# A Fourier filter and MLP mixer: new queues for the first batch's inputs, twelve buffers for the first token weights, and the rounding of weights moved within the prologue

## The chip, the cores and the metric

One core of one Trainium2 chip. The metric is the device time of one execution in microseconds (us), of which several are taken. All executions used below were of the fast state; a ratio is the mean time of one kernel's fast runs over the mean of the other's of the same rounds on the same chip, so it is not quite the ratio of the medians quoted. "Span" is the length of the one execution that was profiled.

## The reference

```python
# x: (8, 3008, 256); filt_r, filt_i: (1505, 256)
X = np.fft.rfft(x, axis=1)
y = np.fft.irfft(X * (filt_r + 1j * filt_i), n=3008, axis=1)      # per channel
# token mixing, then channel mixing; w_tok1 (3008, 256), w_tok2 (256, 3008),
# w_ch1 (256, 1536), w_ch2 (1536, 256)
h = np.maximum(y.transpose(0, 2, 1) @ w_tok1, 0.0) @ w_tok2
u = y + h.transpose(0, 2, 1)
out = u + np.maximum(u @ w_ch1, 0.0) @ w_ch2
```

## The kernel before

The length-3008 transform is split into length-64 and length-47 parts. The first of the eight batches goes through the filter alone, as a prologue; the others are filtered beside the mixer of the batch before. Beside the first batch's filter the weights are also prepared: token weights w1 (twelve tiles) and w2 (twelve tiles), and the channel weights, are loaded into staging buffers and rounded, each in three steps (`begin` loads, `copy` and `end` round).

```python
BY_PE = 6       # so many w2 tiles are added up by TensorE (identity matmuls), the rest on VectorE
EARLY = 12

def filt_load(c, first):                       # the filter pieces of table c
    q = nc.gpsimd if first else nc.sync
    for src, i, p0 in ((filt_r, 0, 0), (filt_i, 1, HALF)) + (...):
        q.dma_start(t[p0:p0 + A, i], raw(src, k0, ...))
        # ... three more pieces on q

early = [(up, "u")] * 2 + [(tp, "t")] * 2 + [(vp, "v")] * 2
late = [(t2p, "t2"), (t3p, "t3")]
stages = [(t4p, "t4")] * (A // 2) + early * 3 + late * 5   # which buffer stages which weight tile

def convert():                                 # one more weight tile rounded, one more load begun
    ended[0] += 1
    while behind and behind[0][0] < ended[0] - 2:
        behind.pop(0)[1]()
    advance(end); advance(copy); advance(begin)

def x_load(b, c):                              # one input tile, two halves
    where, tag = ((xp, "x"), (tp, "t"), (vp, "v"))[c % 3] if b == 0 else (xp, "x")
    # ... both halves on nc.sync

# prologue: the twelve length-64 units of batch 0, then its filter units
for i, _ in enumerate(dft(GROUPS[0])):
    if i == 0:
        for t, src in ((wai_t, wait_d), (wa, wa_d), (wai, wai_d), (ident, ident_d)):
            nc.scalar.dma_start(t, src)
    if i < NXC:                                # NXC = 12
        if i in (0, 2, 4, 6):  advance(begin)
        if i == 5:             advance(copy)
        if i in (7, 9, 11):    convert()       # three tiles rounded here
    elif (i - NXC) % 3 == 2:   convert()       # and one every third filter unit
    # ...
for i in range(rounds, A // 2 + TC * N2 // NG):
    convert()                                  # the rest; the token sums begin at a given i
    if i == A // 2 + BY_PE - 1:
        sum_up()
        acc = token_sums(0)
h1s[0] = token_relu(acc)
```

## Time and profile before

| | before |
|---|---|
| time, median (range), 4 runs beside the changed kernel | 2587.94 us (2585.22 to 2590.66) |
| span, TensorE busy | 2587.2 us, 97% |
| transposes start / last filter product / token sums start / first mixer sums | 31.14 / 122.15 / 136.93 / 166.40 us |
| first to last filter product ("stage 3") | 72.6 us |
| from the first mixer sums to the end ("the rest") | 2420.8 us |

TensorE is nearly always busy from the first mixer sums on. The prologue is therefore read from left to right, as a row of stages, each with the wait that ends it. The prediction below shows the lines. Below, "first mixer sums" is the first `v<-u` of VectorE, as there.

### The profile page before, as it was taken

The numbers are of one execution on the slowest core, as the hardware profiler recorded it, in microseconds if no ns is written. First come the engines' busy times: TensorE is split into PE (matmuls) and PEld (weight loads), VectorE is DVE, ScalarE is ACT, GpSimd is POOL, SyncE is SP. The second block draws the span as 40 slices with busy tenths as digits, with TensorE's granted clock in tenths as the row PEclk, the third lists the DMA queues.
The fourth block names the chain that finished last, engine by engine and source line by source line (L and its number), as shares of the span: only waits on it lengthen the run. The fifth ranks groups of instructions, "written<-read, shape, count | busy, mean of one in ns | idle before, by whom it ended". The sixth has DMA issues, their size and how long they took to land.

```text
span 2587.2 us, 31459 instructions
## 1 busy us (share of the span) xinstructions
PE 2505.6 (97%) x10952; PEld 2000.9 (77%) x10952; DVE 1816.0 (70%) x3458; ACT 691.2 (27%) x1347; POOL 526.9 (20%) x966
## 2 busy tenths in 40 slices
PE   5989999999999999999999999999999999999998
PEld 2556666788878777888787777788888888888887
DVE  6897888556675888746666788846678577647676
ACT  2433222123221222222321222212222122212222
POOL 3652211111211112112112111121121121211212
PEclk7999999999999999999999999999999999999999
DMA  6964333312232332202232233211232121100001
GB/s 167 232 195 155 109 106 103 106 48 90 90 90 64 88 88 71 80 17 89 90 96 77 75 84 87 80 31 57 90 85 75 50 64 53 25 9 8 17 12 21
DMA packets 151834, 205.20 MB, mean 79 GB/s; under 512 B 34216, under 2 KB 102034, under 8 KB 151676
## 3 DMA queue, kind: packets, MB, share of 16 engines
q1 hardware_dynamic: 81068, 115.65, 15.7%
q0 software_dynamic: 30656, 39.93, 6.4%
q10 hardware_dynamic: 39952, 47.61, 5.7%
q8 instruction: 87, 1.43, 0.2%
q14 instruction: 71, 0.58, 0.1%
HBM read 131.23 MB, written 71.83 MB: 78 GB/s over the span
## 4 chain that ended last, share of the span: by engine, by line
PE 78%; DVE 13%; issue 3%; DMA 3%; ACT 2%; SPq 0%; ACTq 0%; POOL 0%; DVEq 0%; POOLq 0%
PE ps_po L631 26%; PE ps_pg L597 15%; PE ps_pg L613 11%; PE ps_b L540 4%; PE ps_b L557 4%; DVE t L575 3%; DVE hh L575 3%; PE ps_acc L540 2%; PE ps_acc L557 2%; PE ps_acc L494 2%; PE ps_b L562 2%; PE ps_acc L417 2%; DVE u L575 2%; DVE s L575 1%; PE ps_b L470 1%
## 5 line engine op out<-in xcount | busy, mean ns | idle before, releaser
L575 DVE TENSOR_TENSOR hh<-ps_pg,s 128x512 f32<-128x512 f32 (+3 forms) x864 | 482.4, 586 | 624.4 <-ACT s L600 623.8
L676 POOL DMA_DIRECT2D out_dram<-r x757 | 409.8, 550 | 1949.1 <-ACT hh L618 929.0
L618 ACT ACTIVATE hh<-hh 128x512 f32<-128x512 f32 (+1 forms) x576 | 348.0, 621 | 1122.8 <-DVE hh L575 1122.8
L631 PE MATMUL ps_po<-t,wc 128*128 128x256 f32 (+1 forms) x2304 | 535.5, 375 | 5.4 <-DVE t L575 4.6
L631 PEld LDWEIGHTS ps_po<-t,wc 128*128 128x128 f32 x2304 | 434.5, 190 | 132.9 <-issue 53.3
L631 PE MATMUL ps_po<-hh,wc 128*128 128x256 f32 (+1 forms) x1728 | 413.2, 375 | 3.1 <-POOL wc L339 2.8
L597 PE MATMUL ps_pg<-v,wc 128*128 128x256 f32 (+1 forms) x1728 | 413.3, 375 | 0.2
L631 PEld LDWEIGHTS ps_po<-hh,wc 128*128 128x128 f32 x1728 | 327.5, 190 | 42.4 <-POOL wc L339 3.6
L597 PEld LDWEIGHTS ps_pg<-v,wc 128*128 128x128 f32 x1728 | 326.9, 190 | 40.5 <-DVE v L575 3.0
L613 PE MATMUL ps_pg<-u,wc 128*128 128x256 f32 (+1 forms) x1152 | 294.5, 378 | 7.0 <-DVE hh L575 6.5
L575 DVE TENSOR_TENSOR t<-t,hh 128x256 f32<-128x256 f32 (+1 forms) x576 | 242.0, 420 | 19.8
L613 PEld LDWEIGHTS ps_pg<-u,wc 128*128 128x128 f32 x1152 | 216.2, 190 | 43.5 <-DVE hh L575 17.4
L575 DVE TENSOR_TENSOR s<-ps_pg,hh 128x512 f32<-128x512 f32 (+1 forms) x288 | 196.0, 681 | 30.7 <-DVE hh L575 0.9
L575 DVE TENSOR_TENSOR t<-hh 128x512 f32<-128x512 f32 (+1 forms) x288 | 192.7, 669 | 0.6 <-ACT hh L618 0.6
L597 PE MATMUL ps_pg<-u,wc 128*128 128x256 f32 (+1 forms) x576 | 169.9, 377 | 1.6 <-DVE hh L575 1.6
L613 PE MATMUL ps_pg<-v,wc 128*128 128x256 f32 (+1 forms) x576 | 169.2, 375 | 0.0
L600 ACT COPY s<-ps_pg 128x256 f32<-128x256 f32 (+1 forms) x288 | 106.0, 368 | 154.7 <-PE ps_pg L597 151.5
L613 PEld LDWEIGHTS ps_pg<-v,wc 128*128 128x128 f32 x576 | 108.9, 190 | 13.3
L597 PEld LDWEIGHTS ps_pg<-u,wc 128*128 128x128 f32 x576 | 102.7, 191 | 20.3 <-issue 8.8
L540 PE MATMUL ps_b<-t,w 128*128 128x256 f32 x480 | 106.3, 384 | 4.3 <-DMA t<-g_tmp 4.3
L557 PE MATMUL ps_b<-w,h 128*128 128x512 f32 (+1 forms) x232 | 107.8, 587 | 0.0
L540 PEld LDWEIGHTS ps_b<-t,w 128*128 128x128 f32 x480 | 92.2, 192 | 17.9 <-issue 4.0
(102 smaller groups left out, 2251.4 us busy)
## 6 DMA issues: line engine op xcount, KB each, us to landing
g_tmp<-t ACTq DMA_DIRECT2D x128, 192.0 KB
x<-in_x_dram SPq DMA_DIRECT2D x184, 128.0 KB
out_dram<-r POOLq DMA_DIRECT2D x698, 32.0 KB, 1.8
z_tmp<-t ACTq DMA_DIRECT2D x84, 256.0 KB
t<-z_tmp SPq DMA_DIRECT2D x112, 192.0 KB
t<-g_tmp SPq DMA_DIRECT2D x42, 512.0 KB
wb<-wbi_t SPq DMA_DIRECT2D x80, 224.0 KB
filt<-in_filt_r_dram SPq DMA_DIRECT2D x128, 48.0 KB
```

The source lines that it names most:

```text
L417: nc.tensor.matmul(ps, wa0 if b == 0 else wa, xs.pop((b, c)).rearrange("p a d -> p (a d)"), start=True, stop=True)
L494: nc.tensor.matmul(ps[0:KR], wbs[k // WC][:, k % WC, P:], p, start=(i == 0), stop=(i == len(parts) - 1))
L540: nc.tensor.matmul(acc[:, t, :], w1[:, a, ts(t, P)], t4[b, a // TC4][:, a % TC4, :], start=(a == 0 and t == 0), stop=(a == A - 1 and t == ...
L557: nc.tensor.matmul(ps[:, 0:w], h1[:, t, ts(dh, P)], w2[:, t, ds(m * 512, w)], start=(t == 0), stop=False)
L562: nc.tensor.matmul(ps[:, ds(q * P, n)], t4[b, c][:, r, ts(dh, P)], wai[:, 0:n], start=False, stop=(q == 3))
L575: nc.vector.tensor_tensor(out=out, in0=in0, in1=in1, op=op)
L597: nc.tensor.matmul(ps[:, 0:hw], chan[0][:, jp, n, :], mov, start=True, stop=True)
L600: nc.scalar.copy(out=s[:, 0], in_=g[0][:, 0, 0:hw])
L613: nc.tensor.matmul(ps[:, 0:hw], chan[0][:, jp, n, :], mov, start=True, stop=True)
L618: nc.scalar.activation(out=hs, in_=hs, func=AF.Relu)
L631: nc.tensor.matmul(po[i][:, j, 0:hw], chan[1][:, jp, n, :], mov, start=(jp == 0 and first == 1), stop=(jp == JP - 1 and last == 1))
L676: q.dma_start(rows[g, e, :, ds(h * A + 4 * m, n)], blocks[ts(g, CW), h, e, 0:n])
```

## The change

The intent: the first batch's input goes ahead of all else, half of it from ScalarE's queue; twelve buffers let all w1 loads start beside the length-64 units; nothing is rounded there. The filter pieces of the first batch, all on GpSimd before, are split between SyncE and GpSimd; more w2 tiles are added up by TensorE.

```diff
-BY_PE = 6
-EARLY = 12
+BY_PE = 8
+BY_PE_LAST = 3
+BESIDE = 13
 def filt_load(c, first):
-        q = nc.gpsimd if first else nc.sync
         for src, i, p0 in ((filt_r, 0, 0), (filt_i, 1, HALF)) + ...:
+            q = nc.gpsimd if first and i else nc.sync
-    early = [(up, "u")] * 2 + [(tp, "t")] * 2 + [(vp, "v")] * 2
-    late = [(t2p, "t2"), (t3p, "t3")]
-    stages = [(t4p, "t4")] * (A // 2) + early * 3 + late * 5
+    round_ = [(p_, t_) for p_, t_ in ((up, "u"), (tp, "t"), (vp, "v"), (t2p, "t2")) for _ in range(2)]
+    stages = [(t4p, "t4")] * 7 + round_ * 3 + [(t2p, "t2"), (t3p, "t3")] * 5
 def w1_load(i):
-        q = nc.sync if i < EARLY else nc.gpsimd
+        q = nc.sync
 # w2_load
-        if i < BY_PE:
+        if i < BY_PE or i >= TC * N2 // NG - BY_PE_LAST:
 # convert: loads begin by a count, up to 7 (at last 4) ahead, instead of one per call
-        advance(begin)
+        while begun[0] < len(tiles) and begun[0] < ended[0] + (4 if begun[0] >= len(tiles) - len(LAST) else 7):
+            start()
 def x_load(b, c):
-        where, tag = ((xp, "x"), (tp, "t"), (vp, "v"))[c % 3] if b == 0 else (xp, "x")
+        where, tag = ((xp, "x"), (t1p, "t1"), *round_[0::2])[c // 2] if b == 0 else (xp, "x")
+            q = nc.scalar if b == 0 and h else nc.sync
 # dft: the first input is all issued ahead; the three first filter tables follow at once
-        ahead = 3 * XB if first else XB
+        ahead = NXC if first else XB
-            if first and i in (5, 8):
-                w_load(i // 6)
+            if first and i < FB:
+                w_load(i)
 # prologue
-                if i in (0, 2, 4, 6):
-                    advance(begin)
-                if i in (7, 9, 11):
-                    convert()
+                if i >= FB:
+                    for _ in range(2 if i < 6 else 1):
+                        start()
 # ... 13 tiles are rounded evenly beside the filter units; sum_up() also before token_relu
```

More of the change, by code (lines that the diff above doesn't have):

```diff
@@ L378, in advance, with start @@
             next(s, None)
+    begun = [0]
+    def start():
+        advance(begin)
+        begun[0] += 1
     def sum_up():
@@ L405, in x_load @@
             lo = h * A + c * XC
-            nc.sync.dma_start(t[h * HALF:(h + 1) * HALF, 0:n, :], rows[:, lo:lo + n, :])
+            q = nc.scalar if b == 0 and h else nc.sync
+            q.dma_start(t[h * HALF:(h + 1) * HALF, 0:n, :], rows[:, lo:lo + n, :])
             if n < XC:
-                nc.sync.dma_start(t[h * HALF:(h + 1) * HALF, n:XC, :], rows[:, lo:lo + 1, :])
+                q.dma_start(t[h * HALF:(h + 1) * HALF, n:XC, :], rows[:, lo:lo + 1, :])
         xs[b, c] = t
@@ L517, in dft @@
                 b_unit(k)
-                if k % KC == 0 and k // KC + 2 < K2 // KC:
+                if k % KC == 0 and k // KC + 2 < K2 // KC and (k or not first):
                     t2_load(k // KC + 2)
@@ L771 @@
             nc.vector.memset(t, 0.0)
-        rounds = 0
         second = dft(GROUPS[1])
@@ L779 @@
             if i < NXC:
-                if i in (0, 2, 4, 6):
-                    advance(begin)
-                if i == 5:
+                if i >= FB:
+                    for _ in range(2 if i < 6 else 1):
+                        start()
+                if i == NXC - 1:
                     advance(copy)
-                if i in (7, 9, 11):
+            else:
+                k = i - NXC - 2
+                if k >= 0 and (k + 1) * BESIDE // (K2 + 1) > k * BESIDE // (K2 + 1):
                     convert()
-                    rounds += 1
-            else:
-                if (i - NXC) % 3 == 2:
-                    convert()
-                    rounds += 1
-                k = i - NXC - 2
                 if 19 <= k < 25:
@@ L805 @@
         chan.extend((both[:, 0], both[:, 1]))
-        for i in range(rounds, A // 2 + TC * N2 // NG):
+        for i in range(BESIDE, A // 2 + TC * N2 // NG):
             convert()
-            if i - rounds < XB:
+            if i - BESIDE < XB:
                 next(second)
@@ L812 @@
                 acc = token_sums(0)
+        sum_up()
         h1s[0] = token_relu(acc)
```

## The prediction

> **What bounds the kernel now.** I read the page first (busy shares, then the 40 slices), then a table of windows cut at the stages of the start, then the timeline of those stages.
>
> ```profile
> PE 2505.6 (97%) x10952; PEld 2000.9 (77%) x10952; DVE 1816.0 (70%) x3458; ACT 691.2 (27%) x1347; POOL 526.9 (20%) x966
> ...
> PE   5989999999999999999999999999999999999998
> ```
>
> TensorE is busy 97% of 2587 us, and nearly all that is missing lies in the first slices of 65 us each. So the change can win only what the start (the "prologue") wastes; from the first mixer step on, every matmul waits for the one before it, and a later first step is a later end. The windows give the stages; the columns are length, then busy time of PE, PEld, DVE, ACT, POOL, then granted clock, DMA share, GB/s:
>
> ```profile
> 0.00:31.14 31.14, 18.04 (x26) 6.10 (x27) 11.22 (x17) 9.97 (x16) 11.06 (x24) 0.85 0.91 227
> 31.14:48.20 17.06, 1.76 (x4) 0.52 (x2) 17.00 (x16) 1.79 (x3) 0.00 (x0) 0.60 0.49 109
> 48.20:122.15 73.95, 67.59 (x233) 39.41 (x233) 63.57 (x140) 33.04 (x68) 48.14 (x87) 0.97 0.81 209
> 122.15:136.90 14.75, 11.30 (x32) 5.53 (x33) 11.19 (x25) 9.07 (x16) 2.76 (x5) 1.00 1.01 259
> 136.90:159.60 22.70, 22.64 (x96) 19.33 (x96) 21.53 (x46) 4.01 (x7) 10.55 (x20) 0.92 0.84 220
> 159.60:166.40 6.80, 6.14 (x26) 3.61 (x26) 4.81 (x10) 2.91 (x5) 1.07 (x3) 1.00 0.00 1
> 166.40:225.00 58.60, 47.37 (x173) 32.36 (x172) 52.73 (x91) 20.26 (x37) 43.22 (x71) 0.94 0.53 166
> 225.00:2587.00 2362.00, 2330.73 (x10366) 1894.10 (x10366) 1633.96 (x3117) 610.16 (x1195) 410.04 (x758) 1.00 0.24 69
> ```
>
> These are: (1) the twelve length-64 units, with batch 0's input coming in; (2) sixteen transposes on VectorE, TensorE idle; (3) 32 filter units with weight tiles rounded between them; (4) what is left before the token sums; (5) the token sums; (6) the steps up to the mixer's first sums; (7) the mixer's start, paced by VectorE, which still rounds ten weight tiles; (8) the steady mixer. Idle TensorE time is 13 + 15 + 6 + 3.5 us in the first four stages and 11 us in the seventh. All of it is 49 us, under 2% of the time, so a gain over 2% is out of reach.
>
> The timeline shows who ends each stage:
>
> ```profile
> 9.55 0.59 ACT L419 COPY turned<-ps_acc 128x512 f32<-128x512 f32 x1 [2.29 <-DMA wai_t<-wait_t]
> ...
> 28.44 2.04 PE L417 MATMUL ps_acc<-x,turned 128*128 128x512 f32 x2 [2.57 <-DMA x<-in_x_dram]
> ...
> 31.14 17.00 DVE L455 STREAM_TRANSPOSE turned<-turned 128x512 f32<-128x512 f32 x16 [1.87 <-ACT turned L419]
> ...
> 136.93 22.64 PE L540 MATMUL ps_b<-t,w 128*128 128x256 f32 x96 [3.40 <-DMA t<-g_tmp]
> ...
> 159.61 0.60 ACT L546 ACTIVATE h<-ps_b 128x512 f32<-128x512 f32 x1 [5.34 <-PE ps_b L540]
> 160.26 1.98 PE L557 MATMUL ps_acc<-w,h 128*128 128x512 f32 x4 [0.69 <-ACT h L546]
> 166.40 0.92 DVE L575 TENSOR_TENSOR v<-u 128x512 f32<-128x512 f32 x1 [1.75 <-ACT u L564]
> ```
>
> The last input tile reaches TensorE at 28.4; the transposes need all twelve tiles, so they start at 31.1. The token sums start 14.8 us after the last filter product (122.15). The first row shows ScalarE held 2.3 us in its own queue: a transfer that it issues waits for an earlier one to land.
>
> **What the Trainium skill says.** "DMA: Bandwidth & Descriptors", section "Issuing engines are not separate DMA queues": transfers started from several engines run on the same 16 DMA engines, so a second queue saves "the time on the sequencer it takes to initiate the DMA". The trace agrees that there is little more to have: one queue issues 128 KB each 0.64 us, 205 GB/s, and the core moved 247 to 264 GB/s between 10 and 25 us. "TensorE: Matmul & The Clock Gate", "What's actually happening": after an idle window of about 3.4 us the clock halves until it has been busy that long. Here, after 2.97 us idle, the input matmul pair took 2.05 us and two more 1.9 and 2.0, against 1.02 to 1.12 warm; the granted clock from 20 to 25 us was 0.51. "ScalarE: Activation LUTs", "What ACT_TABLE_LOAD costs": about 1283 ns for the load; the trace shows 1.28 us.
>
> **The change, part by part.** The engine-by-engine instruction lists of both kernels, with their waits, give the order; the durations are the trace's.
>
> *Inputs first, on two queues.* The input is 3.1 MB; first data at about 4 us as now, then some 250 GB/s with 0.3 MB of filter beside it: last tile at about 16.5 instead of 28.4. But half of the transfers are now issued by ScalarE, ahead of its table load and of the copies that empty PSUM. In the compiled list each queue has four completion semaphores here: ScalarE's fifth input transfer waits for its first to land, and so on. So ScalarE issues its last one when tile 8 has landed (13.3), ends at 13.9, loads the table (15.2), makes copy 0 (15.8), and then has the four constant tables to issue, which wait for the last input tiles and for a filter piece that the other queue issues behind a 224 KB table: about 18.4 (estimate). Only then do copies 1 to 11 run. TensorE has two banks, so it stands at unit 3 until about 19. Nine units at 0.95 warm are 8.6, plus about 1.2 for a cold restart, plus copy 0.6: transposes start at about **29.5**, not 31.1. Most of the 12 us won in the DMA is given back.
>
> *No rounding there.* Three tiles leave stage 1, where VectorE was idle anyway (11.2 of 31.1 busy). Stage 3 before: 32 units at 1.345 (three products, with gaps) + nine 512-wide roundings at 2.26 + two 377-wide at 1.95 = 67.3, against 72.6 from first product to last, so 5.3 of waits, most for filter pieces on the shared GpSimd queue. After: 43.0 + 12 x 2.26 = 70.2, with filter halves on two queues and the w1 tiles loaded beforehand, so I give it 2.0 of waits: 72.2. Last filter product at 29.5 + 17.0 + 1.4 + 72.2 = **120.1** (before 122.15).
>
> *Twelve buffers.* They take the w1 loads out of stage 3 and let w2 loads start earlier; that is in the 2.0.
>
> *More tiles on TensorE.* Eight w2 tiles must now be rounded between the last product and the token sums instead of five (BY_PE 8, and two fewer done before). Before, the five took 12.25 with 2.9 of waits, and the sums started at 14.8, held by the reload of g_tmp. After: 12.25 + 3 x 1.84 + about 0.7 of further wait on ScalarE's order = 18.5, then the last tile's two matmul pairs, 1.3 to 1.5: **20.0** (+5.2). The sums take 22.7 as before. Behind them TensorE now has three more w2 tiles, 3 x 1.27 = 3.8, and in ScalarE's list their copies, about 1.2, stand before the activation that lets it go on; VectorE saves five additions at 0.85 but is waiting by then. So sums to first mixer step: 6.8 + 5.0 = **11.8**.
>
> Sum: 120.1 + 20.0 + 22.7 + 11.8 = 174.6 against 166.4, **+8.2 us**. Stages 7 and 8 have the same instructions, so the end moves with it: 2588.2 + 8.2 = 2596.
>
> **Rivals.**
> (a) *ScalarE does not hold up stage 1*, because its transfers land sooner than I think, and TensorE follows the arrivals. Transposes at 20 to 22, 8 to 9 us sooner than above: the total is then about 2587, and with no waits in stage 3 about 2585. For it: this is plainly the intent, and DMA busy was 0.91 in that stage with w1 in it. Against it: ScalarE's order and waits, and the 2.29 us that it already lost with only four transfers.
> (b) *VectorE is the only bound after stage 1*, and the work taken from it shows as gain: five additions at 0.85 are 4.3 us. For it: it is busy 86% of stage 3 and 95% of stage 5. Against it: it had 1.75 us to spare at 166.4, and TensorE's in-order queue puts the sums between it and the end. It would make 2584 to 2588.
> (c) *The DMA queues bind instead*: twelve w1 tiles (6.2 MB, 25 us at 250 GB/s) stand before the fourth filter table in the in-order queue, and w2 loads bunch after stage 3. It costs 3 to 6 us more: about 2600.
>
> **Range and chances.** My sum says 2596; the misjudgement I fear most, (a), lies wholly below, and (c) is less likely, so I take **2594 us**, 8 in 10 between **2581 and 2603**. Two per cent would be 52 us, more than all idle time of the start: faster 0.01, same 0.98, slower 0.01.
>
> **What would show it.** In the profile after: last input tile landed at 16 to 18; ScalarE's second copy into the turned tile not before 17; transposes from 28 to 31 (at 22 or earlier, rival a); first to last filter product 72 us with waits of 2 (over 76, rival c); token sums 20 us after the last product; six identity matmul groups between the sums and the activation; VectorE idle before it. If the mixer's first sums come before 166, I am wrong in stage 1 or in the order after the sums; if they come at 174 and the end does not move, the mixer's start had slack that I have not seen.

## The result, and the profile after

The changed kernel takes 2615.56 us (median of 4 runs, 2613.96 to 2616.15) against 2587.94 on the same chip: ratio 1.0106, 95% interval 1.0088 to 1.0123. The class "within 2%" was right. The time was not: 2615.6 lies 12.6 us above the range, and the loss is 27 us where 6 were expected.

The windows of the changed kernel, cut at the same events (columns as in the prediction):

```profile
0.00:30.22 30.22, 16.86 (x24) 5.71 (x24) 4.50 (x5) 8.25 (x14) 6.28 (x15) 1.00 0.87 226
30.22:47.28 17.06, 0.00 (x0) 0.00 (x0) 17.00 (x16) 1.67 (x3) 0.00 (x0) 0.63 0.72 170
47.28:136.08 88.80, 71.56 (x229) 41.72 (x229) 66.66 (x144) 32.70 (x67) 26.23 (x47) 0.88 0.67 174
136.08:154.95 18.87, 18.62 (x49) 8.25 (x50) 14.88 (x34) 11.23 (x20) 4.01 (x8) 1.00 0.89 250
154.95:175.83 20.88, 20.88 (x98) 18.40 (x97) 16.85 (x36) 4.40 (x9) 5.19 (x10) 1.00 0.34 107
175.83:187.09 11.26, 9.94 (x38) 5.53 (x37) 5.84 (x11) 5.64 (x10) 2.71 (x6) 1.00 0.11 33
```

The third row holds the loss. VectorE works 3.1 us more there than before, but the row is 14.9 us longer, and DMA is busy only 0.67 of it: everything waits, and the wire (the 16 DMA engines that all queues share) isn't full. Stage by stage, with the step of the prediction beside it (differences to the kernel before, us):

| stage | predicted | measured |
|---|---|---|
| start of the transposes | -1.6 | -0.9 (30.22) |
| first to last filter product | -0.4 (72.2) | **+14.9 (87.5)** |
| last product to token sums | +5.2 (20.0) | +4.1 (18.9) |
| token sums | 0 | -1.7 (20.9) |
| sums to first mixer sums | +5.0 (11.8) | +4.5 (11.3) |
| first mixer sums to the end | 0 | **+6.5 (2427.3)** |
| span | +8.2 | +27.2 |

Stage 3 first. The waits of the changed kernel between 47 and 136 us; columns: engine and line, what it waited for, us in total, times, longest. First SyncE's queue, then VectorE, then ScalarE, then TensorE:

```profile
SPq L302 <- DMA g_tmp<-t: 23.1, 2, 17.9
...
DVE p L492 <- PE ps_pg L480: 6.3, 5, 2.0
DVE p L492 <- PE ps_b L480: 6.0, 1, 6.0
DVE p L492 <- ACT filt L226: 4.2, 2, 2.4
...
ACT filt L226 <- DMA filt<-in_filt_r_dram: 21.4, 6, 9.2
...
PE ps_b L480 <- DMA wb<-wbi_t: 9.2, 3, 7.4
```

(SyncE's row is of 30 to 136 us.) In the kernel before, the same list has no w1 load that waits for `g_tmp` at all (`L301` is the w1 load there, `L302` here), and shorter waits of VectorE:

```profile
SPq L301 <- DMA st<-in_moe_w_tok_dram: 1.4, 2, 0.7
...
DVE p L482 <- PE ps_pg L470: 2.2, 5, 0.7
DVE p L482 <- ACT filt L225: 2.0, 2, 1.7
```

So a load of weights, which needs nothing but a free buffer, stood for 17.9 us because of the write of a result of the first filter units. The timeline shows what stood behind it: SyncE's queue, then the engines that wanted what it brings.

```profile
30.50 32.91 SPq L302 DMA_DIRECT2D st<-in_moe_w_tok_dram  x11
63.51 0.54 SPq L445 DMA_DIRECT2D wb<-wbi_t  x1
64.16 0.32 SPq L214 DMA_DIRECT2D filt<-in_filt_r_dram  x1
...
53.19 0.33 ACTq L515 DMA_DIRECT2D g_tmp<-t  x1
...
66.63 1.22 PE L480 MATMUL ps_b<-turned,wb 128*128 128x256 f32 x2 [7.45 <-DMA wb<-wbi_t]
...
67.24 0.62 ACT L226 COPY filt<-filt 64x512 f32<-64x512 f32 x1 [9.21 <-DMA filt<-in_filt_r_dram]
```

The last eleven w1 transfers (each tile takes two) keep SyncE 33 us, though one issue takes some 0.5; only then come the fourth filter table (`wb`, 63.51) and its real pieces (64.16), and TensorE and ScalarE stand for 7.5 and 9.2 us. The compiled instruction lists say why a load waits for a result. A transfer reports that it has landed on a completion semaphore. SyncE's loads and ScalarE's writes use the same eight of them, handed out in turn, and each transfer first waits for the one that used its semaphore last:

```
the changed kernel's lists (place, line, transfer, what it waits for)
ScalarE   32 L515 DMACopy g_tmp<-t_304 96x2x256 [waits DMAHW0_49,Activation_49]
ScalarE   36 L515 DMACopy g_tmp<-t_341 96x2x256 [waits DMAHW4_49,Activation_49]
SyncE     44 L302 DMACopy st<-in_moe_w_tok_dram 64x512 [waits DMAHW0_49]
SyncE     48 L302 DMACopy st<-in_moe_w_tok_dram 64x256 [waits DMAHW4_49]
SyncE     49 L445 DMACopy wb<-wbi_t 128x448 [waits DMAHW5_49,PE_49]
```

The trace's instruction records have the same: eight semaphores for the two queues, and SyncE's 46th and 50th transfers (places 44 and 48 of the list) waiting for those that the two `g_tmp` writes count on. Semaphore 0 had gone last to the first `g_tmp` write, which ScalarE issues at 53.19, when the first filter units are done. So load 44, whose turn came at 37.5 when load 43 had been issued, stood until that write had landed, 55.35; in this time the DMA engines were only 0.33 busy, so it isn't the volume that it waits for. Load 48 stood likewise until 62.95 for the second write, issued at 58.06; there they were 0.92 busy, with the four w1 transfers just let go. Behind it comes the fourth filter table, place 49.

The rest next. About 2 of its 6.5 us come in the first 60 us of the mixer (the same step of VectorE comes 1.9 us later than before, counted from the first mixer sums; the second batch's token activation comes 359.0 us after the first batch's, before 357.2); later batches agree. The other 4.3 come after the last output is issued. The last transfers of GpSimd, of the changed kernel:

```profile
2604.34 2.72 POOL L686 DMA_DIRECT2D out_dram<-r  x5 [13.48 <-issue]
```

They end at 2607.06, and the span at 2614.4; in the kernel before they end at 2584.19, and the span at 2587.2. No view of the profile shows work in between. The trace's instruction records, which also hold what the views leave out, have one DRAIN instruction of GpSimd there: 3.08 us long before, 7.42 after. All other engines have finished 4.5 us before it ends; in the kernel before, 0.2 us.

### The profile page after: what moved, and what is told of

Read it like the earlier page. It is cut to its first block, busy times and chain, and to the rows that moved or that the text cites. A ratio compares the mean times of both kernels' runs of the same rounds, so it can differ in the third digit from the quotient of the medians.

```text
span 2614.4 us, 31473 instructions
## 1 busy us (share of the span) xinstructions
PE 2517.4 (96%) x10972; PEld 2008.0 (77%) x10972; DVE 1811.9 (69%) x3451; ACT 694.2 (27%) x1354; POOL 501.5 (19%) x917
## 4 chain that ended last, share of the span: by engine, by line
PE 77%; DVE 14%; issue 3%; DMA 2%; ACT 2%; POOL 1%; ACTq 0%; DVEq 0%; SPq 0%; POOLq 0%
PE ps_po L641 26%; PE ps_pg L607 15%; PE ps_pg L623 11%; PE ps_b L550 4%; PE ps_b L567 4%; DVE t L585 3%; DVE hh L585 3%; PE ps_acc L550 2%; PE ps_acc L567 2%; PE ps_acc L504 2%; PE ps_b L572 2%; PE ps_acc L427 2%; DVE u L585 2%; DVE s L585 2%; PE ps_b L480 1%
## 5 line engine op out<-in xcount | busy, mean ns | idle before, releaser
L504 PE MATMUL ps_acc<-p,wb 128*96 128x256 f32 (+1 forms) x256 | 98.0, 485 | 11.7 <-ACT t L510 5.5
```

Source lines behind the costliest of these rows:

```text
L504: nc.tensor.matmul(ps[0:KR], wbs[k // WC][:, k % WC, P:], p, start=(i == 0), stop=(i == len(parts) - 1))
```

## The experiments

All twelve kernels computed the right result. In the table, "to the end" is the time from the first mixer sums to the end, "GpSimd's transfers" are counted in the trace, and the last column is how long after GpSimd's last transfer its DRAIN ended.

| kernel | median us | ratio to before (95%) | transposes | stage 3 | to sums | after sums | first mixer sums | to the end | GpSimd's transfers | DRAIN |
|---|---|---|---|---|---|---|---|---|---|---|
| before | 2587.9 | | 31.1 | 72.6 | 14.8 | 6.8 | 166.4 | 2420.8 | 901 | 2.2 |
| changed | 2615.6 | 1.0106 (1.0088-1.0123) | 30.2 | 87.5 | 18.9 | 11.3 | 187.1 | 2427.3 | 852 | 6.5 |
| e1 w1 tail on GpSimd | 2606.4 | 1.0063 (1.0048-1.0078) | 29.0 | 75.6 | 18.9 | 11.3 | 174.0 | 2426.4 | 862 | 7.5 |
| e2 old staging buffer | 2613.0 | 1.0093 (1.0078-1.0108) | 30.1 | 84.7 | 18.9 | 11.3 | 184.2 | 2426.0 | 852 | 6.5 |
| e3 input all on SyncE | 2615.7 | 1.0100 (1.0085-1.0115) | 22.7 | 94.4 | 18.6 | 11.3 | 186.2 | 2427.3 | 852 | 6.5 |
| e4 no w2 tile after the sums | 2611.3 | 1.0086 (1.0069-1.0102) | 30.5 | 87.0 | 18.5 | 6.8 | 182.1 | 2425.5 | 852 | 6.5 |
| e6 nine w1 tiles begun | 2605.0 | 1.0063 (1.0048-1.0078) | 30.1 | 77.3 | 18.9 | 11.3 | 176.8 | 2425.7 | 852 | 6.5 |
| e5 four edits | 2610.5 | 1.0082 (1.0067-1.0097) | 32.8 | 83.3 | 18.9 | 6.8 | 181.0 | 2427.4 | 862 | 7.5 |
| e5b, input half on GpSimd | 2595.4 | 1.0030 (1.0014-1.0047) | 20.0 | 78.9 | 18.9 | 6.8 | 163.9 | 2428.9 | 875 | 8.7 |
| e7, six w2 tiles on TensorE | 2610.2 | 1.0081 (1.0066-1.0097) | 32.0 | 82.5 | 15.2 | 11.5 | 180.6 | 2426.8 | 862 | 7.5 |
| e8 real filter halves back | 2598.3 | 1.0042 (1.0027-1.0057) | 29.5 | 73.6 | 18.6 | 11.3 | 172.3 | 2424.4 | 901 | 2.2 |
| e9 = e5b with filters back | 2582.9 | 0.9981 (0.9965-0.9998) | 20.2 | 73.5 | 18.5 | 6.8 | 158.3 | 2422.0 | 924 | 2.8 |
| e10 input on SyncE, nine tiles | 2588.3 | 1.0003 (0.9989-1.0018) | 22.7 | 74.9 | 18.9 | 6.8 | 162.5 | 2424.5 | 901 | 2.2 |
| e11 input half on GpSimd, nine tiles | 2582.7 | 0.9981 (0.9966-0.9996) | 20.5 | 74.9 | 18.9 | 6.8 | 160.4 | 2421.4 | 914 | 2.6 |

The kernel before, run beside them, had medians of 2587.5 to 2589.3 us. Each edit below is against the changed kernel.

**e1: the last five w1 tiles from GpSimd's queue.** Theory: the w1 loads in SyncE's queue are what stage 3 waits for.

```diff
-        q = nc.sync
+        q = nc.sync if i < 7 else nc.gpsimd
```

> The changed kernel with the last five of the twelve w1 tiles loaded from the GpSimd queue, not the SyncE queue. Theory A (shared completion semaphores): the SyncE queue stands for 17.9 us before w1 load 20 and again before load 24, because each takes over the completion semaphore of a g_tmp write that ScalarE issues only after the first filter products; the fourth filter table stands behind them. Without these loads in that queue the gap of 6 to 7 us after the eighth filter product goes, first to last filter product is 80 us or less instead of 87.5, and the total falls by 6 to 12 us. Rival B (the 6.2 MB of w1 simply keep the DMA engines busy): the gap stays within 2 us. Rival C (later stalls around 120 to 131 us have the same cause): then first to last product falls to 76.

Stage 3 fell from 87.5 to 75.6 us and the time by 9.2. The w1 loads that stay in SyncE's queue no longer wait for `g_tmp`, and the longest single wait of a filter product was 1.4 us. The 75.6 is what rival C had named: the later stalls go too. So 12 of the 15 us need the w1 loads in that place; that they need the filter pieces behind them as well is shown by e8.

**e2: the old staging buffer for one w2 tile.** Theory: the time after the first mixer sums is longer because of which buffer stages which late weight tile.

```diff
-    stages = [(t4p, "t4")] * 7 + round_ * 3 + [(t2p, "t2"), (t3p, "t3")] * 5
+    stages = [(t4p, "t4")] * 7 + round_ * 2 + round_[0:6] + [(t3p, "t3")] + [(t2p, "t2"), (t3p, "t3")] * 5
```

> The changed kernel with the staging buffers of the last rounds drawn in another order, so that the first late channel tile is not staged in the buffer that the second channel tile of the early list still holds. Theory D: GpSimd's in-order queue stood 21.8 us for that buffer, issued its channel-weight loads only at 184.4, and its sums for the first channel tiles came 3.9 us later; this is most of the 6.4 us that the mixer's start lost beyond the later first step. Expected: first mixer sums at 187 as in the changed kernel, but the wait of TensorE for GpSimd's sums (3.0 us) gone and the total 3 to 6 us below the changed kernel. Rival: the mixer's start is bound by VectorE anyway and the total stays within 1.5 us.

The theory fell: the rest went from 2427.3 to 2426.0, a fifth of what was to be explained. The wait that it named, TensorE's 3.0 us for GpSimd's sums, did go; a wait of 3.0 us for VectorE took its place, as the rival had it. The time is not distinguishable from the changed kernel's (the intervals overlap).

**e3: the whole first input from SyncE.** Theory: ScalarE's waits for its own input transfers hold up the length-64 units.

```diff
-            q = nc.scalar if b == 0 and h else nc.sync
+            q = nc.sync
```

> The changed kernel with all of the first batch's input on the SyncE queue. Theory E (ScalarE's issuing holds up its own copies): the transposes start at 20 to 22 us instead of 30.2 although the last input tile lands 1 to 3 us later. Rival (TensorE or the DMA engines bound stage 1): transposes at 28 or later. The total need not follow, since the stall of the SyncE queue in the filter units ends with the g_tmp writes: if it keeps its length, the total falls by 7 to 10 us.

The transposes start 7.5 us sooner, 22.72 instead of 30.22, as the theory has it. And nothing is won: stage 3 becomes 94.4, and the first mixer sums come at 186.2 instead of 187.1. TensorE gets the fourth filter table at the same time as in the changed kernel (66.63):

```profile
66.27 1.22 PE L480 MATMUL ps_b<-turned,wb 128*128 128x256 f32 x2 [14.76 <-DMA wb<-wbi_t]
```

TensorE arrives 7.5 us earlier and waits 7.3 us longer. The wait for the semaphore did move: ScalarE issues its second `g_tmp` write at 50.38 instead of 58.06, and SyncE goes on at 54.77 instead of 62.95. But then eight w1 transfers of 256 KB still stand before the table, where the changed kernel had one left:

```profile
54.77 4.94 SPq L302 DMA_DIRECT2D st<-in_moe_w_tok_dram  x8
59.80 0.53 SPq L445 DMA_DIRECT2D wb<-wbi_t  x1
```

The DMA engines are 0.81 busy from 55 to 60 us and fully busy from 60 to 66.3. So here volume took what the shorter wait gave, and that both tables land at the same time is chance. A gain is worth nothing while other loads stand before the transfer that is waited for; this is why stage 1 had to be judged together with stage 3.

**e4: no w2 tile left to TensorE behind the token sums.**

```diff
-BY_PE_LAST = 3
+BY_PE_LAST = 0
```

> The changed kernel with no w2 tile joined on TensorE behind the token sums (BY_PE_LAST 0 instead of 3). Theory F: token sums' end to the mixer's first sums falls from 11.4 to about 7 us, total 3 to 5 us less. Rival: VectorE, with three additions of 0.83 more, becomes the bound there, and the total stays within 1.5 us.

After the sums 6.8 us pass instead of 11.3, so these three tiles cost 4.5 us there. The timelines show it. The changed kernel has six groups of identity matmuls and their copies in ScalarE's order before the activation that starts the next step, at 180.27, 4.4 us after the sums end (175.83). Without them it starts as soon as the sums end (175.32). First the changed kernel, then e4:

```profile
175.67 0.80 PE L285 MATMUL ps_po<-both,ident 128*128 128x377 f32 x2
...
179.66 0.81 ACT L288 COPY w<-ps_po 128x192 f32<-128x192 f32 x2 [0.42 <-PE ps_po L286]
180.27 0.62 ACT L556 ACTIVATE h<-ps_b 128x512 f32<-128x512 f32 x1
```

```profile
175.32 0.60 ACT L556 ACTIVATE h<-ps_b 128x512 f32<-128x512 f32 x1 [5.18 <-PE ps_b L550]
```

**e6: nine w1 tiles begun in stage 1 instead of twelve, the queues unchanged.** Here the rest of the loads come behind the fourth to sixth filter tables. It is to separate the order in the queue from the volume.

```diff
-                    for _ in range(2 if i < 6 else 1):
-                        start()
+                    start()
```

> Only nine instead of twelve w1 tiles are begun beside the length-64 units; no queue is changed. The loads that stood in the in-order SyncE queue behind a busy completion semaphore come later then, after the fourth and fifth filter tables. Theory (order): what costs is that those loads stand ahead of the filter tables while they wait for a semaphore that a slow write of ScalarE's queue holds; then the stall of some 18 us in the SyncE queue is gone or falls where nothing is needed, stage 3 (first to last filter product) is 76 to 79 us instead of 87.5, and the total is 2605 to 2609. Rival (volume): the 6.2 MB of w1 ahead of the tables is what costs, so that three tiles less take away only a quarter of the 15 us: stage 3 is 83 to 85, total 2611 to 2613.

Stage 3 is 77.3, in the range of the order theory and far from that of volume. The same three tiles on the same queue cost 10 us less when they come later.

**e5, e5b, e7: the parts put together.** e5 takes the edits of e1, e2, e3 and e4. e5b has GpSimd in e3's edit (`q = nc.gpsimd if b == 0 and h else nc.sync`). e7 is e5 with `BY_PE = 6`.

> Four edits at once: last five w1 tiles from GpSimd's queue, the old staging buffer for one w2 tile, the whole first input from SyncE, no w2 tile left to TensorE after the sums. If the parts found so far are independent and add up: transposes at 22.7, stage 3 76 us, sums 18.5 after the last product, first mixer sums 6.8 after the sums, so at about 163 (before 166.4), and with the 6.4 us that the rest is longer (2427 against 2421) the total is 2590 (2587 to 2592), level with the kernel before. Rival (each gain is given back in the next stage, as with the input on one queue alone, where 7.5 us won in stage 1 were lost in stage 3): stage 3 is 82 or more, first mixer sums after 169, total 2595 to 2600.

> As the run with four edits, but the second half of the first input is issued by GpSimd instead of SyncE. If ScalarE's waits alone cost stage 1 its 7.5 us, two queues without ScalarE do as well as one or a little better: transposes at 21 to 23, the rest as there, total within 2 us of that run. Rival: GpSimd's queue is slower to issue or its own copies of constants come late, and the transposes start at 25 or later.

> As the run with four edits, and six instead of eight w2 tiles go to TensorE before the token sums. Theory: the 4 us that stage 4 gained are the extra tiles that must be rounded before the sums may start; with two fewer, the sums start 14.5 to 15.5 us after the last product instead of 18.5, and the total is 3 us below that run if VectorE keeps pace. Rival: VectorE's additions for those two tiles come back in the sums, which then last 22.5 instead of 20.9, and behind them, so that the first mixer sums come no sooner than 1 us before that run's.

e5 missed by 20 us: its transposes start at 32.8, not at 22.7. Each edit alone was as expected, and the sum was not. The timeline of TensorE in its stage 1 shows input tiles that arrive late:

```profile
25.78 2.05 PE L427 MATMUL ps_b<-x,turned 128*128 128x512 f32 x2 [1.45 <-DMA x<-in_x_dram]
30.05 2.05 PE L427 MATMUL ps_acc<-x,turned 128*128 128x512 f32 x2 [2.23 <-DMA x<-in_x_dram]
```

In e3 the w1 loads stood behind the input in one queue, the first issued at 24.6 us, so the input had the wire; in e5 GpSimd's otherwise empty queue issues eight w1 transfers between 12.8 and 20.4 us, beside the last input tiles, and they share it. e5b bears this out: with half of the input in front of them in GpSimd's own queue the first w1 transfer there is issued at 17.7, the transposes start at 20.0, and the kernel is 15 us faster, where a difference of at most 2 was expected. In e7 two tiles fewer save 3.7 us before the token sums, as expected, and VectorE, which then must do their additions, loses 4.7 after them: TensorE's next step waits 2.77 us for a w2 tile (`w`) from VectorE and then runs slower for a while (the same eight small matmuls take 1.91 us, 1.05 in e5). The sums themselves stay at 20.9, not at the rival's 22.5. So the two tiles are worth nothing either way (e7 is 0.3 us from e5).

**e8: the real halves of the first filters back on GpSimd.** This undoes one line of the change.

```diff
-            q = nc.gpsimd if first and i else nc.sync
+            q = nc.gpsimd if first else nc.sync
```

> The changed kernel with the real halves of the first batch's filters back on GpSimd, so that GpSimd issues 901 transfers as in the kernel before (the changed one 852). The silent tail at the end is one DRAIN instruction on GpSimd; it ended 2.2 us after GpSimd's last transfer at 901 transfers, and 6.5, 7.5 and 8.7 us after it at 852, 862 and 875 (0.097 us for each), whatever else differed. Theory (count): it depends on the number of transfers that GpSimd issued alone, so it is 2.2 here and the time from the first mixer sums to the end falls from 2427.3 to about 2423. Rival: it belongs to something else in the changed program, and stays at 6.5. For stage 3: if the w1 loads in SyncE's queue are all that hurts, first to last product stays at about 87; if the filter pieces behind them in that queue are what is waited for, it falls to 80 or less, and the total to 2600 or less.

This one line is 17.3 us of the 27 (2615.6 to 2598.3). Stage 3 is 73.6 us, and SyncE still stands:

```profile
SPq L445 <- PE ps_acc L504: 39.3, 11, 5.8
...
SPq L302 <- DMA g_tmp<-t: 15.3, 1, 15.3
...
DVE p L492 <- PE ps_b L480: 1.4, 1, 1.4
```

The w1 load waits 15.3 us for its semaphore, nearly as in the changed kernel, but VectorE's longest wait is 1.4 us, for what stands behind it isn't needed yet: the filter pieces are in another queue, and SyncE reaches the fourth filter table earlier:

```profile
30.37 24.76 SPq L302 DMA_DIRECT2D st<-in_moe_w_tok_dram  x8
55.23 14.62 SPq L445 DMA_DIRECT2D wb<-wbi_t  x5
```

The tail shrank too: the DRAIN ends 2.2 us after the last transfer, as the count theory had it. "To the end" is 2424.4 instead of 2427.3, not 2423, for the mixer's start came out slower here (as in e10, some 3 us more than before in its first 60 us; why isn't shown).

**e9, e10, e11: what the parts make together without that line.** e9 is e5b with e8's edit. e10 has the edits of e3, e4, e6 and e8; e11 is e10 with half of the input on GpSimd.

> The best run so far (second half of the first input and five w1 tiles on GpSimd, old staging buffer, no w2 tile after the sums) with the real filter halves on GpSimd too: 924 transfers on GpSimd. Count theory: the DRAIN ends 2.2 to 4.5 us after the last transfer instead of 8.7. If stage 3 stays at 79 us, the total is 2589 to 2592; the shared GpSimd queue may cost stage 3 up to 5 us (the filters then stand behind the input half), 2594 to 2597.

> Whole first input on SyncE, only nine w1 tiles begun in stage 1, no w2 tile after the sums, real filter halves on GpSimd (901 transfers there). Transposes at 22.7, stage 3 at 76 to 78, sums 18.5 to 18.9 after the last product, 6.8 after them: first mixer sums at 164 to 166. With the rest at 2421 to 2423 the span is 2586 to 2589, level with the kernel before (2587.2). Rival: stage 3 gives back what stage 1 gains and lasts 82 or more; span above 2592.

> As the run before it, but the second half of the first input on GpSimd (914 transfers there). Transposes at 20 to 21; stage 3 at 76 to 80; first mixer sums at 162 to 166; DRAIN 2.2 to 3.5 us after the last transfer; span 2584 to 2589. Rival: the filter pieces stand behind the input half in GpSimd's queue and stage 3 lasts 83 or more.

e9 and e11 are the fastest: 2582.9 and 2582.7 us, ratio 0.9981, with both intervals just below 1. They beat the kernel before by 0.2% and the changed one by about 1.2%. Both came out faster than expected: in both I had feared that filter pieces behind the input half would cost stage 3, and it lasts 73.5 and 74.9. e10 came out level, as expected, but partly by luck: its stage 3 was shorter than expected (74.9) and its rest longer (2424.5). The first mixer sums come 8.1 us earlier in e9 than before, and the span is 6.8 shorter: now the prologue's gain does reach the end.

## Why the prediction was wrong

**Stage 1, right in the mechanism.** "So ScalarE issues its last one when tile 8 has landed (13.3), ends at 13.9, loads the table (15.2), makes copy 0 (15.8)", then four issues and the other copies "about 18.4". ScalarE and TensorE in the changed kernel:

```profile
13.04 0.54 ACTq L419 DMA_DIRECT2D x<-in_x_dram  x1
13.62 1.28 ACT L429 ACT_TABLE_LOAD   x1 [13.62 <-DMA x<-in_x_dram]
...
17.89 0.59 ACT L429 COPY turned<-ps_acc 128x512 f32<-128x512 f32 x1 [2.39 <-DMA wa<-wa_t]
...
15.55 2.07 PE L427 MATMUL ps_b<-x,turned 128*128 128x512 f32 x2 [7.24 <-DMA x<-in_x_dram]
18.53 2.07 PE L427 MATMUL ps_acc<-x,turned 128*128 128x512 f32 x2 [0.91 <-ACT turned L429]
```

Copy 1 at 17.89 and unit 3 at 18.53 against 18.4 and 19. The transposes came at 30.2 and not 29.5 because I gave 1.2 us to the cold restart; the four units from 18.53 on took 2.07, 1.91, 1.92 and 1.30 against 1.02 warm, so some 3 us. Rival (a), that ScalarE doesn't hold up stage 1, is refuted by e3: without it the transposes start at 22.7.

**Stage 3, the step that failed.** "After: 43.0 + 12 x 2.26 = 70.2, with filter halves on two queues and the w1 tiles loaded beforehand, so I give it 2.0 of waits". The 70.2 is not contradicted: e8 and e9 last 73.6 and 73.5. The waits were 17.3, not 2.0. Both reasons I named for few waits are what made them: the two-queue split put the real halves into SyncE's in-order queue, and the twelve w1 tiles stood before the later ones. e1, e6 and e8 each take away one part of the collision, and stage 3 falls to 75.6, 77.3 and 73.6. Rival (c) had this place and this queue, but sized it by volume ("6.2 MB, 25 us at 250 GB/s") at 3 to 6 us. The longest wait is a matter of order: a load waited for a semaphore that was to be released by a write not yet issued, with the DMA engines 0.33 busy. Volume adds to it, in the second wait and in e3. The root lies in the reading of the list: "In the compiled list each queue has four completion semaphores here: ScalarE's fifth input transfer waits for its first to land". In the trace there are eight that both queues share, and ScalarE's fifth transfer waits for the semaphore of SyncE's first. With four of its own, SyncE's queue could not have waited for a ScalarE write in this way. I didn't follow SyncE's waits down its own list, where they stand.

**Before the token sums and behind them, right.** 18.9 against 20.0, and 11.3 against 11.8. e4 shows the latter's cost by itself, e7 the former's. Rival (b), that VectorE's work taken away shows as gain, fell too. The sums did shorten by 1.7 us (22.6 to 20.9), which I had put at none, but not for VectorE's sake: e7, in which VectorE has all its additions back, has 20.9 as well. The windows show the granted clock at 0.92 in the sums before and at 1.00 after. The kernel before had waited 3.40 us for `g_tmp` first, and its clock record is at one half from 137.58 for 3.4 us, which makes the 1.7.

**"Stages 7 and 8 have the same instructions, so the end moves with it", wrong by 6.5.** 4.3 us of it are GpSimd's DRAIN. Its end is the same in kernels with the same number of GpSimd transfers, whatever else differs: five kernels with 852 have 6.5, three with 862 have 7.5, one with 875 has 8.7, and three with 901 have 2.2; for e8 this was forecast before it ran. 914 and 924 have 2.6 and 2.8. So it grows by some 0.096 us a transfer, has fallen back somewhere between 875 and 901, and grows again by 0.02 to 0.03; where and why is not shown. It isn't in proportion to the bytes that GpSimd moved (38.4, 40.9 and 42.5 MB at 852, 862 and 875); which transfers count was not separated. The change took 49 transfers off GpSimd and thereby came to the wrong side. The remaining 2.2 us lie mostly in the mixer's first 60 us and were not traced further.

**What stays open**: the rule behind the DRAIN; the 2.2 us (0.2 to 3.3 in the other kernels); and the 4 us by which stage 3 varies between e1, e6 and e8, whose w1 loads and filter pieces are placed differently.

## What to carry to other kernels

A transfer moved to another queue takes its place in an order: ask what stands before it there and what each of those waits for, its completion semaphore too, which may be held by a write that another engine has yet to issue. Transfers that aren't urgent belong behind the urgent ones in the same queue, neither before them (the changed kernel) nor at the front of an empty one (e5). And undo each line of a change by itself before you believe in its main idea: here most of the idea was sound (e9, e11, which issue half of the input from GpSimd instead of ScalarE and leave no w2 tile behind the sums), and one line beside it cost 17 of the 27 us. Such shares don't add up: moving the w1 loads instead (e1, e6) won about 10 of the same us.

## What the Trainium skill lacked or had wrong

- "DMA: Bandwidth & Descriptors", section "Issuing engines are not separate DMA queues": a second issuing engine is said to save only the time to initiate transfers. The runs agree about the wire, but the section lacks that it can cost much more than it saves: with half of the input on ScalarE the transposes started at 30.2 us, with all of it on SyncE at 22.7 (e3), since ScalarE's own copies stood behind its issues. It also lacks that two queues which share completion semaphores can hold each other up: a SyncE load stood 17.9 us for a ScalarE write that was issued 16 us after the load was ready.
- No page has a DRAIN of GpSimd at the end of a program that lasts microseconds: 3.1 to 9.6 us long here, some 0.096 us more for each GpSimd transfer between 852 and 875 of them, and 3.1 to 3.7 us at 901 to 924.
- "TensorE: Matmul & The Clock Gate", section "What's actually happening": the clock is said to halve after an idle window of about 3.4 us. The window need not be empty: in the kernel before, the clock record goes to one half at 18.11, 28.36 and 35.18 us, each time after 3.41 us in which TensorE had still worked for 0.9 to 1.1 us. The changed kernel doesn't contradict the section: after 7.24 us idle its matmul pairs took 2.07 to 1.91 us until 23.8 and 1.02 from 24.94, and its clock record begins only at 24.35, with the full clock, so that the 1.00 of the windows before that isn't a measurement.
- "ScalarE: Activation LUTs", section "What ACT_TABLE_LOAD costs", agrees: 1283 ns there, 1.28 us here.
